# A decode kernel's 30 attention units: written out, and as a loop of 15 rounds

## The chip, the cores and the metric

The kernel runs on one core of one Trainium2 chip. The core has five engines that run side by side, each with its own instruction queue: TensorE (PE, matrix multiplies; its weight loads are listed as PEld), VectorE (DVE), ScalarE (ACT), GpSimd (POOL) and SyncE (SP, which here only issues loads and stores). Sixteen DMA engines move data between HBM and the on-chip memory. The metric is device time in microseconds (us), the median of several runs: 1339.32 us before the change (three runs, 1339.19 to 1339.5).

## What is computed

One decode step: an attention block over a long key/value cache and a small MLP block on the same input, mixed by a gate. Cut to what matters:

```python
def reference(A_x, A_k_cache, A_v_cache, A_wq, A_wo, B_x, B_w1, ..., gate_w):
    # x: (2, 1, 1024); k_cache, v_cache: (2, 32, 16384, 128); wq: (1024, 4096); wo: (4096, 1024)
    x = A_x
    g = sigmoid((x * gate_w).sum(-1, keepdims=True))
    q = (x @ wq) split into 32 heads of 128
    p = softmax(einsum("bhqd,bhkd->bhqk", q, k_cache) * 128 ** -0.5)
    a = einsum("bhqk,bhkd->bhqd", p, v_cache) joined over heads @ wo
    b = x1 + gelu(layernorm(x1) @ w3) @ w4      # x1 = x + shifted gelu(layernorm(x) @ w1) @ w2
    return g * a + (1 - g) * b
```

All inputs are bf16. K and V are 268 MB each, and every byte of them is read once.

## The kernel before

**Units.** The attention is cut into 32 units. A unit is a pair of heads `hp` (0 to 15) of one batch row `b` (0 or 1), in the order `units` (line 88): unit u is pair u // 2 of batch u % 2. Its K is 8 MB and its V is 8 MB, each loaded by one DMA of 128 rows of 64 KB (`load_k`, line 96; `load_v`, line 99).

**Memory.** One tile `mem` of five cells of 32 KB per partition holds the caches: K of even units in cells 0 and 1, K of odd units in cells 1 and 2, V in cells 3 and 4. So the next K may be loaded when the half of the current K that lies in the shared cell 1 has been used, and the next V when the current V has been used. V of unit 30 goes to cells 0 and 1, since no K follows there.

**One unit's work.** `write_qw` (291, POOL) writes the query into a zero-padded weight tile. `score_chunks` (446) goes over K in eight chunks: DVE transposes a chunk (line 454, tile KT, two buffers), PE multiplies it (line 460, 8 matmuls a chunk, into S). `score_first` takes the half in the shared cell, `score_second` the other. `softmax_a` (478) transposes S and takes maxima; `softmax_b` (488) joins the maxima over a matmul and takes exponentials on ACT into the tile Pt; `softmax_c` (509) sums and inverts into rinv. `pv` (543) multiplies Pt with V, 64 matmuls on line 535; `pv_end` (567) scales, reduces, and stores the result in OT; for batch 1 it also projects the pair with `wo` (`wo_project`, line 430), adding to `arow` in PSUM.

**The order.** The loop over units (line 623) is a Python loop, so it is written out in full in the program. In turn n it issues: score_first(n); the load of K(n+1); score_second(n); softmax_a(n); pv(n-2); the load of V(n-1); pv_end(n-2); softmax_b(n); softmax_c(n); and in every fourth turn the `wo` rows of two pairs (`load_wo_pair`, 418). Turns 0 and 1 have pieces of the MLP in place of pv. The last turn loads V of unit 31 in nine pieces (`load_v_pieces`, 105), and `wo` of the last two pairs in four loads (`load_wo_last`, 424). After it come pv and pv_end of unit 30, `pv_last` of unit 31 (595), and the output (663 to 666). A scheduler places waits on semaphores and may move an instruction ahead of others of its engine when it is ready sooner. All loads are issued from SP, in order, on one queue.

Of the kernel before, what the change touches and what calls it, by code (L numbers as in the profile page):

```python
# [1 line left out]

# [1 line left out]

# [7 lines left out]
BF16 = mybir.dt.bfloat16  # L12
ACTF = mybir.ActivationFunctionType
ALU = mybir.AluOpType
# [9 lines left out]
def kernel(  # L24
# [65 lines left out]
    def cache_rows(cache, u):  # L90
# [2 lines left out]
            "(p j) d -> p (j d)", p=P  # L93
        )

    def load_k(u):
        nc.sync.dma_start(out=region(k_cell[u], NJ * Dh), in_=cache_rows(A_k_cache, u))

# [18 lines left out]
    def v_view(u):  # L117
        return region(v_cell[u], NJ * Dh).rearrange("p (j d) -> p j d", d=Dh)
# [169 lines left out]
    lin3.load()  # L288
    qdu = qd[:].rearrange("p hp b v -> p (hp b) v")

    def write_qw(u):
        t = qw[u % NW]
        dst = t[:, :, NG - 1 : NG - 1 + QP * (Q4 - 1) + 1 : QP]
        nc.gpsimd.tensor_tensor(  # L294
            out=dst,
            in0=qdu[:, u, :].unsqueeze(2).to_broadcast([P, 4, Q4]),
            in1=mask4[:].unsqueeze(1).to_broadcast([P, 4, Q4]),
            op=ALU.mult,
        )
# [102 lines left out]

    OT = const.tile([P, HP, 2, B], BF16)
    LASTP = 2
    wo_pairs = A_wo.rearrange("(hp p r) n -> p hp (r n)", p=P, r=2)
    wo_heads = A_wo.rearrange("(h d) n -> d h n", d=Dh)
    wo_tiles = {}

    def wo_tile(hp0):
        t = wopool.tile([P, 2, 2, D], BF16, name="wo")
        for k in range(2):
            for r in range(2):
                wo_tiles[hp0 + k, r] = t[:, k, r, :]
        return t

    def load_wo_pair(hp0):
        t = wo_tile(hp0)
        nc.sync.dma_start(  # L420
            out=t[:].rearrange("p k r n -> p k (r n)"), in_=wo_pairs[:, hp0 : hp0 + 2, :]
        )

    def load_wo_last():
        t = wo_tile(HP - LASTP)
        for k in range(2):
            for r in range(2):
                nc.sync.dma_start(out=t[:, k, r, :], in_=wo_heads[:, H - 4 + 2 * k + r, :])

    def wo_project(hp):  # L430
        for r in range(2):
            for k in range(NH2):
                nc.tensor.matmul(  # L433
                    arow[k],
                    lhsT=OT[:, hp, r, :],
                    rhs=wo_tiles[hp, r][:, k * 512 : (k + 1) * 512],
                    start=False,
                    stop=(hp == HP - 1 and r == 1),
                    skip_group_check=True,
                )  # L440

    S_tiles = {}
    st_tiles = {}
# [2 lines left out]
    def score_chunks(u, chunks, first, last):  # L446
        if first:
            S_tiles[u] = sps.tile([P, GT * QP], FP32, name="S")
        S = S_tiles[u][:].rearrange("p (j k) -> p j k", k=QP)
        t = qw[u % NW]  # L450
        for n, c in enumerate(chunks):
            Kc = k_view(u)[:, c * CT : (c + 1) * CT, :]
            kt = ktpool.tile([P, CT * Dh // 2], FP32, name="KT")
            nc.vector.transpose(out=kt[:], in_=Kc.rearrange("p j d -> p (j d)").bitcast(FP32))  # L454
            ktb = kt[:].bitcast(BF16).rearrange("p (j w k e) -> p j w k e", j=CT, w=2, k=QP, e=2)
            for half in range(CT // GT):
                m = c * (CT // GT) + half
                for v in range(4):
                    w, e = divmod(v, 2)
                    nc.tensor.matmul(  # L460
                        S,
                        lhsT=t[:, v, NG - 1 - m : NG - 1 - m + P],
                        rhs=ktb[:, half * GT : (half + 1) * GT, w, :, e],
                        start=(first and n == 0 and half == 0 and v == 0),
                        stop=(last and n == len(chunks) - 1 and half == CT // GT - 1 and v == 3),
                    )
# [1 line left out]

    half_chunks = [list(range(NCK // 2)), list(range(NCK // 2, NCK))]

    def score_first(u):
        write_qw(u)
        score_chunks(u, half_chunks[1 - k_cell[u]], True, False)

    def score_second(u):
# [12 lines left out]
    def softmax_b(u):  # L488
        st, Dm = st_tiles.pop(u)
        R_ps = misc_psum([P, P])  # L490
        nc.tensor.matmul(R_ps[:], lhsT=ones_f[:], rhs=Dm[:], start=True, stop=True)  # L491
# [15 lines left out]
        rs_tiles[u] = rs  # L507
# [22 lines left out]

    def pv_moving(u, g0, g1, ng):
        acc = oacc[u % 2]
        for g in range(g0, g1):
            q = g % Q4
            nc.tensor.matmul(  # L535
                acc[QP * q : QP * q + 8, :],
                lhsT=pts[u % NP][:, g].rearrange("p h k -> p (h k)"),
                rhs=v_view(u)[:, 4 * g : 4 * g + 4, :].rearrange("p j d -> p (j d)"),
                start=(g < Q4),
                stop=(g >= ng - Q4),  # L540
            )

    def pv(u):
        pv_moving(u, 0, NJ // 4, NJ // 4)
# [22 lines left out]
    def pv_end(u):  # L567
        hp, b = units[u]
        mask = stat.tile([P, 4], FP32, name="maskr")
        nc.vector.tensor_scalar(  # L570
            out=mask[:], in0=mask4m[:], scalar1=rinvs[u % NP][:, 0:1],
            scalar2=g_rep[:, b : b + 1], op0=ALU.mult, op1=ALU.mult,
        )
        red = pv_rows(u, mask)
        if hp >= HP - LASTP:
            ot = misc_psum([P, 2])
            nc.tensor.matmul(ot[:], lhsT=red[:, 0:Dh], rhs=hsel[:], start=True, stop=True)
            nc.vector.tensor_copy(out=OT[:, hp, :, b], in_=ot[:])
            return
        ot = misc_psum([P, 2, 2])  # L580
        for r in range(2):
            nc.tensor.matmul(  # L582
                ot[:, r, :],
                lhsT=red[:, r : 2 * Dh : 2],
                rhs=hsel[:],
                start=True,
                stop=True,
            )
        for e in range(2):
            rows = slice(e * HALF, (e + 1) * HALF)  # L590
            nc.vector.tensor_copy(out=OT[rows, hp, :, b], in_=ot[rows, :, e])  # L591
        if b == B - 1:
            wo_project(hp)

    def pv_last(u):
        hp, b = units[u]
# [5 lines left out]
        for j in range(4 * moving, NJ):  # L602
# [4 lines left out]
                start=(j == 4 * moving),  # L607
                stop=False,
            )
        for k in range(HP - LASTP, HP - 1):  # L610
            wo_project(k)
        nc.tensor.matmul(ot[:], lhsT=red[:, 0:Dh], rhs=hsel[:], start=False, stop=True)
        nc.vector.tensor_tensor(out=OT[:, hp, :, b], in0=ot[:], in1=rinvs[u % NP][:], op=ALU.mult)
        wo_project(HP - 1)

    compute_gate()
    layernorm_T(xT[:], xn1T[:], "ln1")
# [2 lines left out]
    lin2.compute()  # L620
    mlp_post2()

    for n in range(NU):
        score_first(n)
        if n + 1 < NU:
            load_k(n + 1)
        else:
            load_v(NU - 2)
        score_second(n)
        softmax_a(n)  # L630
        if n == 0:
            load_wo_pair(0)
# [5 lines left out]
        elif n == 1:  # L638
# [5 lines left out]
        else:  # L644
            pv(n - 2)
            if n < NU - 1:
                load_v(n - 1)
            else:
                load_v_pieces(NU - 1)
            pv_end(n - 2)  # L650
            if n == NU - 1:
                load_wo_last()
            softmax_b(n)
            softmax_c(n)
        if n % 4 == 1 and 1 < n < NU - 3:
            load_wo_pair((n - 1) // 2)
    pv(NU - 2)
    pv_end(NU - 2)
    pv_last(NU - 1)

    out_row = mlp.tile([QP + B, 512], BF16)
    rows = out.rearrange("b s d -> (b s) d")
    nc.vector.tensor_copy(out=out_row[0:B, :], in_=arow[0])  # L663
    nc.sync.dma_start(out=rows[:, 0:512], in_=out_row[0:B, :])
    nc.scalar.activation(out=out_row[QP : QP + B, :], in_=arow[1], func=ACTF.Copy)
    nc.scalar.dma_start(out=rows[:, 512:1024], in_=out_row[QP : QP + B, :])


# [28 lines left out]
```

## Time and profile before

| | |
|---|---|
| median of 3 runs | 1339.32 us |
| the profiled execution: its time | 1339.11 us |
| the profiled execution: its span | 1337.4 us |
| HBM read | 572.53 MB, 428 GB/s over the span |
| granted TensorE clock, mean | 0.776 |
| K loads, issue to landing (median of 32) | 28.3 us |
| V loads, issue to landing (median of 31) | 33.3 us |

How to read the rows that follow: "busy us, mean ns, idle before, releaser" tells how long a group of instructions ran, how long one took, and what ended the idle time of its engine before it. In a timeline each row has its start and its length in us from the start of the span, the engine, the line and the operation, out<-in, and in brackets the idle time before it. SPq is SP's queue, where DMAs are issued. "q1" and so on are DMA queues: q1 carries the data, q8 and q14 carry instructions to the engines; their rows have packets, MB and the share of 16 engines' span. A row of a chain has start, length and what ran. A row of windows has a stretch, its length, busy time and count of PE, PEld, DVE, ACT and POOL, then the granted clock, the busy share of the DMA engines and GB/s.

### The profile page before, as it was taken

How to read it: one execution, taken by the hardware profiler on the slowest of the kernel's cores; microseconds unless marked ns; L12 is line 12 of the kernel's file. 1: busy time of each engine (PE TensorE's matmuls, PEld its weight loads, DVE VectorE, ACT ScalarE, POOL GpSimd, SP SyncE). 2: the span in 40 equal slices, each digit the busy share in tenths (PEclk: the TensorE clock that was granted, in tenths of full speed). 3: DMA queues.
4: the chain of work that ended last, by engine and by line, in shares of the span. 5: the costliest groups of instructions: out<-in, count | busy, mean ns of one | idle time of the engine just before them, and what ended most of it. 6: DMA issues, size and time to landing. Idle time of an engine off the chain costs nothing.

```text
span 1337.4 us, 11166 instructions
## 1 busy us (share of the span) xinstructions
PE 753.6 (56%) x4842; PEld 314.7 (24%) x4842; DVE 711.9 (53%) x700; ACT 106.9 (8%) x169; POOL 13.9 (1%) x49
## 2 busy tenths in 40 slices
PE   2456566554566645556655546665455765545664
PEld 1223222221222222222222212222222222222221
DVE  2455566553556654456555445656455665545561
ACT  0011000000000000000000000000000000000000
POOL 1000000000000000000000000000000000000000
PEclk9678888776788767788777778877678887778886
DMA  9999999999999999999999999999999999999997
GB/s 408 436 423 440 428 434 432 436 426 437 434 430 440 423 434 432 438 438 420 438 424 438 436 434 434 420 435 430 441 428 432 436 422 430 436 436 432 426 431 321
DMA packets 14041, 573.25 MB, mean 429 GB/s; under 512 B 1828, under 2 KB 1832, under 8 KB 4392
## 3 DMA queue, kind: packets, MB, share of 16 engines
q1 hardware_dynamic: 13988, 572.54, 99.4%
q8 instruction: 38, 0.62, 0.2%
q14 instruction: 11, 0.09, 0.0%
q10 hardware_dynamic: 4, 0.00, 0.0%
HBM read 572.53 MB, written 0.00 MB: 428 GB/s over the span
## 4 chain that ended last, share of the span: by engine, by line
DMA 73%; PE 12%; DVE 12%; issue 4%; SPq 0%
DMA mem<-in_A_k_cache_dram 70%; DVE KT L454 11%; PE S L460 11%; DMA mem<-in_A_v_cache_dram 2%; DMA wo<-in_A_wo_dram 1%; PE oacc L535 0%; SPq L217 0%; DVE out_row L663 0%; PE arow L433 0%; SPq L125 0%; SPq L123 0%; SPq L121 0%
## 5 line engine op out<-in xcount | busy, mean ns | idle before, releaser
L460 PE MATMUL S<-KT,qw 128*128 128x512 bf16 x2048 | 548.4, 418 | 385.8 <-DVE KT L454 385.4
L454 DVE STREAM_TRANSPOSE KT<-mem 128x2048 f32<-128x2048 f32 x256 | 570.9, 2282 | 285.2 <-DMA mem<-in_A_k_cache_dram 234.6
L460 PEld LDWEIGHTS <-qw 128*128 128x128 bf16 x2048 | 219.0, 107 | 710.4 <-issue 531.9
L535 PE MATMUL oacc<-mem,pt 128*8 128x512 bf16 x2040 | 120.1, 387 | 13.3 <-DMA mem<-in_A_v_cache_dram 13.3
L499 ACT ACTIVATE pt<-St,nb 64x256 bf16<-64x256 f32 x64 | 89.7, 1402 | 151.8 <-DVE nb L497 150.9
L485 ACT ACTIVATE Dm<-ident_s,m 128x128 f32<-128x128 f32 x32 | 12.9, 402 | 1003.0 <-DVE m L483 1003.0
L513 PE MATMUL misc<-rs,lmat 128*128 128x1 f32 x62 | 18.2, 363 | 87.7 <-ACT pt L499 87.7
L535 PEld LDWEIGHTS <-pt 128*8 128x8 bf16 x2040 | 47.3, 87 | 82.4 <-issue 31.6
L515 DVE RECIPROCAL rinv<-misc 128x1 f32<-128x1 f32 x31 | 5.2, 168 | 100.1 <-PE misc L513 100.1
L481 DVE STREAM_TRANSPOSE St<-S 128x512 f32<-128x512 f32 x32 | 22.9, 717 | 65.6 <-PE S L460 65.6
L551 DVE TENSOR_SCALAR part<-oacc,maskr 128x128 f32<-128x128 f32 x31 | 10.9, 351 | 83.1 <-PE oacc L535 83.1
L582 PE MATMUL misc<-hsel,red 128*128 128x2 f32 x112 | 17.2, 258 | 51.6 <-DVE red L557 51.6
L513 PEld LDWEIGHTS misc<-rs,lmat 128*128 128x128 f32 x62 | 15.5, 311 | 101.6 <-ACT pt L499 101.6
L582 PEld LDWEIGHTS misc<-hsel,red 128*128 128x128 f32 x112 | 15.6, 199 | 64.9 <-issue 64.9
L499 ACT ACTIVATION_READ_ACCUMULATOR pt<-St,nb 64x1 f32 x64 | 30.5, 477 | 0.0
L557 DVE SCALAR_TENSOR_TENSOR part<-oacc,maskr,part 128x128 f32<-128x128 f32 x62 | 21.8, 351 | 2.2
L274 PE MATMUL oacc<-mem,xT 128*2 128x512 bf16 x128 | 8.3, 426 | 23.4 <-DVE xT L265 23.4
L591 DVE CAST OT<-misc 64x2 bf16<-64x2 f32 x56 | 9.0, 160 | 22.7 <-PE misc L582 22.3
L294 POOL TENSOR_TENSOR qw<-qd,mask 128x16 bf16<-128x16 bf16 x32 | 8.5, 267 | 1189.0 <-PE S L460 1165.9
L491 PE MATMUL misc<-Dm,ones_f 128*128 128x128 f32 x64 | 16.7, 346 | 1.8 <-ACT Dm L485 1.8
L497 DVE TENSOR_REDUCE nb<-misc 64x1 f32<-64x64 f32 x64 | 14.2, 222 | 4.6 <-PE misc L491 2.9
L557 DVE SCALAR_TENSOR_TENSOR red<-oacc,maskr,part 128x256 f32<-128x256 f32 x31 | 15.0, 484 | 1.1
(97 smaller groups left out, 114.4 us busy)
## 6 DMA issues: line engine op xcount, KB each, us to landing
mem<-in_B_w_dram SPq DMA_DIRECT2D x2, 7168.0 KB, 35.1
wo<-in_A_wo_dram SPq DMA_DIRECT2D x7, 1024.0 KB, 31.8
mem<-in_A_v_cache_dram SPq DMA_DIRECT2D x7, 1024.0 KB, 23.5
mem<-in_B_w_dram SPq DMA_DIRECT2D x2, 2048.0 KB, 31.2
mem<-in_A_v_cache_dram SPq DMA_DIRECT2D x2, 512.0 KB, 17.9
wo<-in_A_wo_dram SPq DMA_DIRECT2D x4, 256.0 KB, 12.8
mem<-in_A_k_cache_dram SPq DMA_DIRECT2D x32, 28.3
mem<-in_A_v_cache_dram SPq DMA_DIRECT2D x31, 33.3
```

Of the source, the lines that this page charges most:

```text
L454: nc.vector.transpose(out=kt[:], in_=Kc.rearrange("p j d -> p (j d)").bitcast(FP32))
L460: nc.tensor.matmul(S, lhsT=t[:, v, NG - 1 - m : NG - 1 - m + P], rhs=ktb[:, half * GT : (half + 1) * GT, w, :, e], start=(first and n == 0 ...
L481: nc.vector.transpose(out=st[:].rearrange("p j r -> p (j r)"), in_=S[:])
L485: nc.scalar.activation(out=Dm[:], in_=ident_s[:], func=ACTF.Copy, scale=m[:, 0:1])
L491: nc.tensor.matmul(R_ps[:], lhsT=ones_f[:], rhs=Dm[:], start=True, stop=True)
L497: nc.vector.tensor_reduce(out=nb[rows], in_=R_ps[rows, rows], axis=AX.X, op=ALU.min)
L499: nc.scalar.activation(out=Pt[rows, :, e, :].rearrange("p (m a) k -> p a k m", a=GT // 4), in_=st[rows, :, 0:NG].rearrange("p (a k) m -> p ...
L513: nc.tensor.matmul(tot_ps[:, 0:1], lhsT=lmat[:], rhs=rs[:], start=True, stop=True)
L535: nc.tensor.matmul(acc[QP * q : QP * q + 8, :], lhsT=pts[u % NP][:, g].rearrange("p h k -> p (h k)"), rhs=v_view(u)[:, 4 * g : 4 * g + 4, ...
L551: nc.vector.tensor_scalar(out=part[:], in0=acc[:, 0:Dh], scalar1=mask[:, 0:1], scalar2=None, op0=ALU.mult)
L557: nc.vector.scalar_tensor_tensor(out=red[:] if twice else part[:], in0=in0.unsqueeze(1).to_broadcast([P, 2, Dh]) if twice else in0, scalar ...
L582: nc.tensor.matmul(ot[:, r, :], lhsT=red[:, r : 2 * Dh : 2], rhs=hsel[:], start=True, stop=True,)
```

## The change

Units 0 and 1 stay written out. Units 2 to 31 become a loop of 15 rounds on the chip, i from 0 to 14, with a register as counter. A round has two units: 2 + 2i, and 3 + 2i. The second unit stands in an `If`: in rounds 0 to 13 the first arm runs it; in round 14 the `Else` arm runs unit 31 with all that followed the loop before, the output too. With `iteration_sync="reg_based"` the loop does not stop the engines between rounds to reset semaphores: the semaphores only grow, and a wait in the body compares with a register that is raised in each round. `hint_engines=()` asks for no branch hints.

```diff
+    pairs = {
+        "k": [cache_pairs(A_k_cache, b) for b in range(B)],
+        "v": [cache_pairs(A_v_cache, b) for b in range(B)],
+    }
+    def load_pair(cell, cache, hp, b):
+        src = pairs[cache][b][bass.ds(hp, 1)].rearrange("o p x -> (o p) x")
+        nc.sync.dma_start(out=region(cell, NJ * Dh), in_=src)
...
-    NP = 4
+    NP = 2
...
-    def write_qw(u):
+    def write_qw(u, at=None):
         t = qw[u % NW]
+        q = qdu[:, u, :] if at is None else qdu[:, bass.ds(at, 1), :].rearrange("p o v -> p (o v)")
...
-    OT = const.tile([P, HP, 2, B], BF16)
-    LASTP = 2
+    OT = const.tile([P, 2, B], BF16, name="OT")
+    OT_last = const.tile([P, 2, B], BF16, name="OT_last")
...
+    wo_now = wopool.tile([P, 2, D], BF16, name="wo")
+    def load_wo(hp):
+        src = wo_pairs[hp] if isinstance(hp, int) else wo_pairs[bass.ds(hp, 1)].rearrange(
+            "o p x -> (o p) x"
+        )
+        nc.sync.dma_start(out=wo_now[:].rearrange("p r n -> p (r n)"), in_=src)
     def load_wo_last():
-        t = wo_tile(HP - LASTP)
-        for k in range(2):
-            for r in range(2):
-                nc.sync.dma_start(out=t[:, k, r, :], in_=wo_heads[:, H - 4 + 2 * k + r, :])
+        for r in range(2):
+            nc.sync.dma_start(out=wo_now[:, r, :], in_=wo_heads[:, H - 2 + r, :])
...
+    queued = [None]
+    def behind():
+        return tc.issue_after(queued[0].ins) if queued[0] is not None else nullcontext()
...
-    for n in range(NU):
+    for n in range(2):
...
+    def unit_first(b, i):
+        u = 2 + b
+        score_first(u, 2 * i + u)
+    def unit_second(b):
+        u = 2 + b
+        score_second(u)
+        softmax_a(u)
+        pv(b)
+    def unit_end(b):
+        u = 2 + b
+        pv_end(b)
+        softmax_b(u)
+        softmax_c(u)
...
+    with tc.For_i(0, HP - 1, 1, hint_engines=(), iteration_sync="reg_based") as i:
+        queued[0] = None
+        unit_first(0, i)
+        load_pair(k_cell[1], "k", i + 1, 1)
+        unit_second(0)
+        load_pair(v_cell[1], "v", i, 1)
+        unit_end(0)
+        with tc.If(i < HP - 2) as more:
+            queued[0] = None
+            unit_first(1, i)
+            nxt = nc.s_assert_within(
+                i + 2, 2, HP - 1, skip_runtime_bounds_check_because="this arm has i < HP - 2"
+            )
+            load_pair(k_cell[2], "k", nxt, 0)
+            unit_second(1)
+            load_pair(v_cell[2], "v", i + 1, 0)
+            unit_end(1)
+            load_wo(i + 1)
+        with more.Else():
+            n = NU - 1
+            queued[0] = None
+            score_first(n)
+            load_v(n - 1)
+            score_second(n)
+            softmax_a(n)
+            pv(n - 2)
+            load_v_pieces(n)
+            pv_end(n - 2)
+            load_wo_last()
+            softmax_b(n)
+            softmax_c(n)
+            pv(n - 1)
+            pv_end(n - 1)
+            pv_last(n)
+            nc.vector.tensor_copy(out=out_row[0:B, :], in_=arow[0])
...
```

With it come four smaller edits. The addresses of K, V and `wo` in HBM, and of the query, are worked out from the counter (`load_pair`, `load_wo`, `write_qw`); K and V are viewed by pairs of heads, with the same 128 rows of 64 KB. `wo` is loaded one pair at a time, in each round, into one tile; the last pair alone is loaded in the order by heads, in two loads. Pt and rinv have two buffers instead of four, and OT one pair. The matmuls of `pv_moving`, and softmax_b's, are pinned behind the last matmul queued on PE before them (`behind`), where before the scheduler's own order held.

More of the change, by code (lines that the diff above doesn't have):

```diff
@@ L1 @@
-from contextlib import ExitStack
+from contextlib import ExitStack, nullcontext
 import numpy as np
@@ L459, in score_chunks @@
                     w, e = divmod(v, 2)
-                    nc.tensor.matmul(
+                    queued[0] = nc.tensor.matmul(
                         S,
@@ L490, in softmax_b @@
         R_ps = misc_psum([P, P])
-        nc.tensor.matmul(R_ps[:], lhsT=ones_f[:], rhs=Dm[:], start=True, stop=True)
+        with behind():
+            nc.tensor.matmul(R_ps[:], lhsT=ones_f[:], rhs=Dm[:], start=True, stop=True)
         nb = stat.tile([P, 1], FP32, name="nb")
@@ L532, in pv_moving @@
         acc = oacc[u % 2]
[L533 to L541, printed above, removed]
+        with behind():
+            for g in range(g0, g1):
+                q = g % Q4
+                last = nc.tensor.matmul(
+                    acc[QP * q : QP * q + 8, :],
+                    lhsT=pts[u % NP][:, g].rearrange("p h k -> p (h k)"),
+                    rhs=v_view(u)[:, 4 * g : 4 * g + 4, :].rearrange("p j d -> p (j d)"),
+                    start=(g < Q4),
+                    stop=(g >= ng - Q4),
+                )
+        queued[0] = last
     def pv(u):
@@ L590, in pv_end @@
             rows = slice(e * HALF, (e + 1) * HALF)
[L591 removed]
+            nc.vector.tensor_copy(out=OT[rows, :, b], in_=ot[rows, :, e])
         if b == B - 1:
[L593 removed]
+            wo_project(OT, wo_now)
     def pv_last(u):
@@ L637 @@
             softmax_c(n)
-        elif n == 1:
+        else:
             lin4.compute()
@@ L662 @@
[L662 to L666, printed above, removed]
+            pv(n - 1)
+            pv_end(n - 1)
+            pv_last(n)
+            nc.vector.tensor_copy(out=out_row[0:B, :], in_=arow[0])
+            nc.sync.dma_start(out=rows[:, 0:512], in_=out_row[0:B, :])
@@ L670 @@
+            nc.scalar.activation(out=out_row[QP : QP + B, :], in_=arow[1], func=ACTF.Copy)
+            nc.scalar.dma_start(out=rows[:, 512:1024], in_=out_row[QP : QP + B, :])
 _INS = ['A_x', 'A_k_cache', 'A_v_cache', 'A_wq', 'A_wo', 'B_x', 'B_w1', 'B_w2', 'B_w3', 'B_w4', 'gate_w']
```

63 lines of the change are left out of this document (20 added, 43 removed).

## The prediction

> **What bounds the kernel now.** I read the page's head, its slices and DMA queues first, then the chain that ended last, then one unit in the order of time.
>
> ```profile
> span 1337.4 us, 11166 instructions
> ...
> PE 753.6 (56%) x4842; PEld 314.7 (24%) x4842; DVE 711.9 (53%) x700; ACT 106.9 (8%) x169; POOL 13.9 (1%) x49
> ...
> DMA  9999999999999999999999999999999999999997
> ...
> q1 hardware_dynamic: 13988, 572.54, 99.4%
> q8 instruction: 38, 0.62, 0.2%
> q14 instruction: 11, 0.09, 0.0%
> ...
> DMA mem<-in_A_k_cache_dram 70%; DVE KT L454 11%; PE S L460 11%; DMA mem<-in_A_v_cache_dram 2%; DMA wo<-in_A_wo_dram 1%; PE oacc L535 0%; SPq L217 0%; DVE out_row L663 0%; PE arow L433 0%; SPq L125 0%; SPq L123 0%; SPq L121 0%
> ```
>
> The data queue q1 keeps all 16 DMA engines busy for 99.4% of the span, and the chain is mostly the landing of K. No compute engine passes 56%. So an edit counts if it changes the work of the DMA engines, or if it is late enough to leave their queue empty. How late that is shows in one unit (issue and landing of its loads, and the work between):
>
> ```profile
> 903.75 0.33 SPq L100 DMA_DIRECT2D mem<-in_A_v_cache_dram  x1
> ...
> 907.62 0.38 SPq L420 DMA_DIRECT2D wo<-in_A_wo_dram  x1
> ...
> 917.40 4.50 DVE L454 STREAM_TRANSPOSE KT<-mem 128x2048 f32<-128x2048 f32 x2 [6.58 <-DMA mem<-in_A_k_cache_dram]
> ...
> 927.90 0.33 SPq L97 DMA_DIRECT2D mem<-in_A_k_cache_dram  x1
> ...
> 942.20 0.33 SPq L100 DMA_DIRECT2D mem<-in_A_v_cache_dram  x1
> ...
> 949.47 0.29 DVE L570 TENSOR_SCALAR maskr<-mask4m,rinv,g_rep 128x4 f32<-128x4 f32 x1
> 958.73 4.50 DVE L454 STREAM_TRANSPOSE KT<-mem 128x2048 f32<-128x2048 f32 x2 [8.98 <-DMA mem<-in_A_k_cache_dram]
> 961.10 5.37 PE L460 MATMUL S<-KT,qw 128*128 128x512 bf16 x16 [11.87 <-DVE KT L454]
> ```
>
> ```profile
> mem<-in_A_v_cache_dram SPq DMA_DIRECT2D x31, 33.3
> ```
>
> K lands at 917.40, the work on it ends at 949.76 (949.47 + 0.29), so it takes 32.4 us, and DVE then idles 8.98 us until the next K. There is a second cover behind that: the next K load is issued at 927.90, while the V load issued at 903.75 lands at about 903.75 + 33.3 = 937.05. For 9.15 us the queue still has data, and a K load may be that late before a DMA engine starves. For the V load it is 958.73 - 942.20 = 16.5 us.
>
> How even is the pace? The starts of the first transpose after each K landing, in the chain:
>
> ```profile
> 128.60 2.32 DVE KT L454
> ...
> 403.61 2.32 DVE KT L454
> ...
> 442.31 2.32 DVE KT L454
> ...
> 483.60 2.32 DVE KT L454
> ...
> 561.02 2.32 DVE KT L454
> ...
> 600.96 2.32 DVE KT L454
> ...
> 838.64 2.32 DVE KT L454
> ...
> 878.50 2.32 DVE KT L454
> ...
> 1154.88 2.32 DVE KT L454
> ...
> 1194.74 2.32 DVE KT L454
> ...
> 1272.44 2.32 DVE KT L454
> ```
>
> The DMA queues and loads between 128.60 and 1272.44, and the instructions before, in and after that stretch:
>
> ```profile
> q8 instruction: 32, 0.52, 0.2%
> ...
> wo<-in_A_wo_dram SPq DMA_DIRECT2D x6, 1024.0 KB, 32.1
> ```
>
> ```profile
> 0.00:128.60 128.60, 59.73 (x546) 27.66 (x547) 56.03 (x90) 10.05 (x18) 6.38 (x21) 0.81 0.99 425
> 128.60:1272.44 1143.84, 656.80 (x3998) 272.52 (x3998) 630.12 (x580) 93.06 (x145) 7.48 (x28) 0.77 1.00 432
> 1272.44:1337.40 64.96, 37.02 (x298) 14.49 (x297) 25.76 (x31) 3.79 (x6) 0.00 (x0) 0.74 0.89 375
> ```
>
> A plain unit takes 442.31 - 403.61 = 38.70 us, one with a wo load 483.60 - 442.31 = 41.29, or 2.59 more. Units 2 to 31 start 29 units apart: 29 x 38.70 + 6 x 2.59 = 1137.8, against 1143.84 measured. **6.0 us are left over**, and not evenly: 561.02 to 600.96 is 39.94, 838.64 to 878.50 is 39.86, 1154.88 to 1194.74 is 39.86, three steps of about 1.2 us, 278 and 316 us apart. Those are candidates for instruction fetch. The first two columns of counts are PE's matmuls and weight loads: 9684 instructions in all, and 9684 / 38 packets is 255 per packet of q8, so q8 carries PE's program, one packet every 35 us. Eight packets are 282 us, about the distance of the steps: I read it as one DMA engine receiving every eighth packet and landing its share of K and V later each time. A packet costs that engine 0.2% x 16 x 1337.4 / 38 = 1.13 us (0.84 to 1.41 with the rounding of 0.2%), which is the size of a step. A K load has landed when its slowest engine has, so the steps add up.
>
> **The change, part by part.** *Instructions removed from the stream.* Units 2 to 30 hold 7996 PE instructions, 276 per unit, 551 per round, 2.2 packets. In the loop each round runs the same code. If PE keeps it after the first round, fetches are 1093 / 256 = 4.3 for the start, 2.2 for one round and 595 / 256 = 2.3 for the other arm: about 9 instead of 38, and about 30 of the stretch's 32 are gone. By share of the left-over that is 6.0 x 30 / 32 = 5.6 us; by the visible steps alone 3 x 1.2 = 3.6, or 2.4 if one of the last arm's fetches brings a step back. I take the middle of 3.6 and 5.6, rounded down, **-4.5 us**, ends -2.4 and -6.0. If PE does not keep it, see the rivals.
>
> *Loop control* (counter, compare, two taken branches per round and engine, register additions, addresses for SP and POOL). No row shows one. Lower end 0; upper end by the nearest small instruction, L570's 0.29 us: 30 per round are 8.7 us on an engine. A taken branch may wait for code: 1.13 us of packet at least, at most also a 2 KB transfer's whole trip (the output's issue at 1335.02 to the end at 1337.4, 2.4 us): 3.5 each, 7 per round.
>
> ```profile
> 1335.02 0.33 SPq L664 DMA_DIRECT2D out_dram<-out_row  x1
> ```
>
> I take 0 for the end time, because it falls where DVE idles 8.98 us and PE 11.87 before the next K, 38.70 - 32.4 = 6.3 in a unit without a wo load, and the K load can then slip 9.15 more. Both ends added, 8.7 + 7 = 15.7, just use up 6.3 + 9.15 = 15.4; with that cover gone each us more costs 15. What is late in such a case is first the transpose, then the K load, then on SP's queue the V load and the wo load behind it.
>
> *Waits against registers.* They replace waits on constants at the same places if they are as exact. Behind a waiting K load on SP stand V and wo; behind a waiting transpose on DVE stands the rest of its chain. Exact: 0. Inexact: a rival.
>
> *Loads.* K and V keep their rows, size, cells and order. Seven wo loads of 1 MB and four of 256 KB become fifteen of 512 KB and two of 256 KB: the same bytes, 6 more issues at 0.38 us on an SP that is idle from 907.62 to 927.90. 0.
>
> *Two Pt and rinv buffers instead of four, and PE's order pinned behind the last queued matmul.* The exponentials of a unit already come after PV of the unit two before (V's issue at 942.20 follows that PV). maskr may move from 949.47 into the next unit: 0.29 us in DVE's idle time. 0.
>
> *The end.* Four projection matmuls leave the tail, but the chain there hangs on the last wo load (1% of the span), and the bytes ahead of it are the same. Between 0 and -1.1 (half of the last projections' 2.27); I take 0, since the load comes last.
>
> ```profile
> 1332.01 2.27 PE L433 MATMUL arow<-wo,OT 128*2 128x512 bf16 x8
> ```
>
> Sum: the profiled execution took 1339.11 (span 1337.4 and 1.7 around it), and the median is 1339.32, 0.2 above. 1339.3 - 4.5 = **1334.8 us**.
>
> [...]
>
> **The rivals.** (1) *Fetch stays as it is*: each round fetches its 2 to 3 blocks anew, hidden as now. For it: q8 runs at one packet per 256 instructions all through, so nothing in this trace shows code being kept. Nothing else changes: 1337 to 1341, about 1339.
>
> [...]
>
> (3) *Waits across rounds are coarser*: a K load that waits for the V load ahead of it leaves the queue empty from 937.05 for the trip of a new load, about 2.4 us. Once per round +36, 1375; in each unit +70, 1409. For it: the arms of a branch must meet in one state. Against it: a counter per engine can be exact.
>
> (4) *Control eats the cover*: over 15.4 us per round end; 3 us more give +45, 1384. Against it: that needs both upper ends at once.
>
> **How the numbers follow.** Forecast 0.45, rival 1 0.17, rival 2 0.23, rival 3 0.10, rival 4 0.05. The forecast's own range is 1333 to 1337. The whole range runs to rival 2's 1352 with room for a few more packets, 1332.8 to 1356; rivals 3 and 4 are left out. A measurement of this kernel can tell about 0.2%, 2.7 us, so faster means below 1336.6: nearly all of the forecast, 0.42. Same takes the forecast's upper edge and rival 1, 0.20. Slower, above 1342, takes the rest, 0.38.
>
> **What would show it.** Right: q8 with about 9 to 12 packets, K landings 38.70 apart without steps, q1 still at 99% or more, DVE's idle time before K still there at each round's end. Wrong: q8 at 38 or more (rivals 1, 2), a K landing later than 38.7 once per round, or a slice of the DMA row below 9 in the loop (rivals 3, 4).

## The result, and the profile after

| | median us | lowest to highest, runs |
|---|---|---|
| before | 1339.32 | 1339.15 to 1339.84, 11 |
| after | 1335.85 | 1335.69 to 1336.59, 11 |

The ratio is 0.9974, with a 95% interval of 0.9965 to 0.9984: 3.5 us faster. The forecast was 1334.8. The profiled execution after the change has a span of 1334.2 us, 3.2 less than before. Its page:

```profile
span 1334.2 us, 13326 instructions
...
PE 761.0 (57%) x4846; PEld 321.2 (24%) x4846; DVE 709.0 (53%) x702; ACT 107.0 (8%) x169; POOL 12.8 (1%) x47
...
q1 hardware_dynamic: 13956, 572.54, 99.5%
q8 instruction: 11, 0.18, 0.1%
```

The DMA engines are as full as before, and the engines do the same work but for the loop's control. What has gone is code on its way to PE: 11 packets in place of 38 (before, 9684 / 38 is 255 PE instructions to a packet). When they come is told by the DMA queues in three stretches, 0 to 210 us, 210 to 1290 and 1290 to the end (packets, MB, share):

```profile
q8 instruction: 8, 0.13, 0.3%
```

```profile
q1 hardware_dynamic: 9920, 467.67, 100.2%
```

```profile
q8 instruction: 3, 0.05, 0.4%
```

The middle answer has no row for q8 at all. From 210 us on, 5 us into the second of the 15 rounds, PE runs up to the last arm without one packet of code, and that arm, which no round has run before, brings three. The pace of K in the chain of waits, one row per round (rows between are left out):

```profile
362.81 2.32 DVE KT L467
...
441.48 2.32 DVE KT L467
...
834.90 2.32 DVE KT L467
...
913.58 2.32 DVE KT L467
...
1268.20 2.32 DVE KT L467
```

A round takes 441.48 - 362.81 = 78.67 us, and 78.68 half a millisecond later. Two plain units and half a wo load of before are 2 x 38.70 + 1.30 = 78.70. The steps are gone, and the loop's own control is not to be seen in the pace. The first row after that jump back, in the order of time, shows why:

```profile
913.58 4.50 DVE L467 STREAM_TRANSPOSE KT<-mem 128x2048 f32<-128x2048 f32 x2 [5.94 <-DMA mem<-in_A_k_cache_dram]
```

DVE still stands idle for 5.94 us across the jump back (in brackets), and what ends that is the landing of K, not the jump. Then the middle stretch and the end (length, then busy time and count of PE, PEld, DVE, ACT, POOL, then clock, DMA share, GB/s), with PE's code and the wo loads of the middle one, from its DMA view:

```profile
127.56:1268.20 1140.64, 663.95 (x4000) 278.82 (x4000) 627.32 (x581) 93.05 (x145) 7.43 (x28) 0.77 1.00 433
1268.20:1334.20 66.00, 37.66 (x300) 15.10 (x299) 26.33 (x34) 3.79 (x6) 0.00 (x0) 0.71 0.87 370
```

```profile
q8 instruction: 4, 0.07, 0.0%
...
wo<-in_A_wo_dram SPq DMA_DIRECT2D x14, 512.0 KB, 29.4
```

| stretch | before | after | difference |
|---|---|---|---|
| start to the K of unit 2 | 128.60 | 127.56 | -1.04 |
| K of unit 2 to K of unit 31 | 1143.84 | 1140.64 | -3.20 |
| K of unit 31 to the end | 64.96 | 66.00 | +1.04 |

By the pace worked out for before (38.70 a plain unit, 2.59 per MB of wo) the middle stretch would take 29 x 38.70 + 14 x 1.295 = 1140.4. So of the 6.0 us that were left over before, 0.2 remain. But 7 MB of wo lie in the stretch now and 6 did before, which gives 2.6 back. The end is longer. Its last rows after, and the matching two before:

```profile
1327.94 0.59 PE L619 MATMUL misc<-pt,mem 128*128 128x2 bf16 x16 [0.66 <-DMA mem<-in_A_v_cache_dram]
...
1330.43 0.68 DVE L712 CAST out_row<-arow 2x512 bf16<-2x512 f32 x1 [1.16 <-PE arow L440]
...
1331.14 0.34 SPq L713 DMA_DIRECT2D out_dram<-out_row  x1
```

```profile
1331.07 0.58 PE L603 MATMUL misc<-pt,mem 128*128 128x2 bf16 x16 [0.69 <-DMA mem<-in_A_v_cache_dram]
...
1334.31 0.68 DVE L663 CAST out_row<-arow 2x512 bf16<-2x512 f32 x1 [2.03 <-PE arow L433]
```

From the last K to the last piece of V: 58.63 before (1331.07 - 1272.44), 59.74 after, +1.11. From there to the cast: 3.24 and 2.49, -0.75. From the cast to the end: 3.09 and 3.77, +0.68. Three theories were to be told apart: the gain is code that is no longer fetched; the gain comes from one of the small edits; and, for the end, the arm's own code or the loop's exit brings something back.

### The profile page after: what moved, and what is told of

The parts are those of the page before. It is cut to its first block, busy times and chain, and to the rows that moved or that the text cites. A ratio compares the mean times of both kernels' runs of the same rounds, so it can differ in the third digit from the quotient of the medians.

```text
span 1334.2 us, 13326 instructions
## 1 busy us (share of the span) xinstructions
PE 761.0 (57%) x4846; PEld 321.2 (24%) x4846; DVE 709.0 (53%) x702; ACT 107.0 (8%) x169; POOL 12.8 (1%) x47
## 3 DMA queue, kind: packets, MB, share of 16 engines
q1 hardware_dynamic: 13956, 572.54, 99.5%
## 4 chain that ended last, share of the span: by engine, by line
DMA 65%; PE 13%; DVE 11%; issue 6%; another core or an unknown queue 1%; PEld 0%; DVEq 0%; SPq 0%; PEldq 0%; POOL 0%
DMA mem<-in_A_k_cache_dram 61%; PE S L473 12%; DVE KT L467 11%; DMA mem<-in_A_v_cache_dram 3%; PE oacc L550 1%; PEld L473 0%; DVEq L467 0%; DVE part L573 0%; SPq L109 0%; PE arow L440 0%; DVE red L573 0%; PEld misc L598 0%; DVE part L567 0%; POOL ln_rstd L359 0%
## 5 line engine op out<-in xcount | busy, mean ns | idle before, releaser
L473 PEld LDWEIGHTS <-qw 128*128 128x128 bf16 x2048 | 216.1, 106 | 687.1 <-issue 510.0
L598 PE MATMUL misc<-hsel,red 128*128 128x2 f32 x120 | 20.3, 274 | 70.8 <-DVE red L573 70.8
L598 PEld LDWEIGHTS misc<-hsel,red 128*128 128x128 f32 x120 | 18.6, 219 | 85.1 <-issue 85.1
L505 PE MATMUL misc<-Dm,ones_f 128*128 128x128 f32 x64 | 19.8, 403 | 1.8 <-ACT Dm L498 1.8
L511 DVE TENSOR_REDUCE nb<-misc 64x1 f32<-64x64 f32 x64 | 14.2, 222 | 6.8 <-PE misc L505 3.5
```

The lines of the kernel that those rows point to most:

```text
L473: queued[0] = nc.tensor.matmul(S, lhsT=t[:, v, NG - 1 - m : NG - 1 - m + P], rhs=ktb[:, half * GT : (half + 1) * GT, w, :, e], start=(firs ...
L598: nc.tensor.matmul(ot[:, r, :], lhsT=red[:, r : 2 * Dh : 2], rhs=hsel[:], start=True, stop=True,)
```

## The experiments

Times of the kernel before in these runs were 1339.25, 1339.21 and 1339.19, so the runs can be set side by side.

**The small edits without the loop.** All of the change, but with the rounds written out.

```diff
-    with tc.For_i(0, HP - 1, 1, hint_engines=(), iteration_sync="reg_based") as i:
+    for i in range(HP - 1):
...
-        with tc.If(i < HP - 2) as more:
+        if i < HP - 2:
...
-        with more.Else():
+        else:
```

> The 15 rounds written out again, with every other edit of the change kept (loads by pairs, one wo pair per round, two Pt buffers, PE's order pinned). Fetch theory (the gain is the instruction packets of PE that no longer pass through the DMA engines): q8 back at about 38 packets, steps of about 1.2 us in the K landings, 1339 us, between 1338.3 and 1340. Rival, the smaller edits made the gain: q8 at 38 and still 1336 us.

Measured: 1339.77, ratio 1.0003 (0.9994 to 1.0012). The page's row of PE's code, the windows (split at the K of units 2 and 31), and two rows of the chain:

```profile
q8 instruction: 38, 0.62, 0.2%
```

```profile
127.49:1273.87 1146.38, 654.24 (x4000) 271.95 (x4000) 630.20 (x580) 93.02 (x145) 7.46 (x28) 0.78 1.00 432
1273.87:1338.00 64.13, 37.64 (x300) 14.85 (x299) 25.93 (x32) 3.80 (x6) 0.00 (x0) 0.71 0.87 366
```

```profile
837.46 2.32 DVE KT L467
...
917.29 2.32 DVE KT L467
```

This kernel has the same loads in the same stretch as the changed one, the same work on every engine but for the loop's control, and 38 packets. Its middle stretch is 1146.38 - 1140.64 = **5.74 us longer**. And the steps are back: the round shown takes 79.83 us (917.29 - 837.46), where the loop has 78.67. The gain is the loop's, and the small edits together cost 1338.0 - 1337.4 = 0.6 us of span: -1.1 in the start and -0.8 in the end, where less wo lies, and +2.5 in the middle, where more does.

**What a packet costs, and rounds with twice the code.** Two kernels get 128 tiny matmuls (2x2, into a spare PSUM tile) more in each unit from 2 to 30: one with the rounds written out, one in the loop. The expectations take 0.19 us a packet, the 6.0 us left over in the middle stretch of before by its 32 packets.

```diff
+    def dummies():
+        t = misc_psum([2, 2])
+        with behind():
+            for _ in range(128):
+                nc.tensor.matmul(t[:], lhsT=mask4[:, 0:2], rhs=mask4[:, 0:2], start=True, stop=True)
...
     def unit_end(b):
...
         softmax_c(u)
+        dummies()
```

Written out:

> The written-out rounds with 128 tiny matmuls (2x2) more on PE at the end of each of units 2 to 30: 7424 PE instructions more, 29 packets, into a scratch tile that nothing reads. Fetch theory: q8 at about 67 and 29 x 0.19 = 5.5 us more than the same without them, about 1344.5 (1342 to 1348). Rival, PE's time counts and not the packets: it is off by what the same matmuls cost in the loop.

In the loop:

> The changed kernel (loop) with the same 128 tiny matmuls more at the end of each of units 2 to 30. They run on PE as often as in the written-out kernel, but stand in the program once per unit of a round, 2 packets. Fetch theory: q8 at 12 to 15, 1336 to 1337 us, since PE idles some 9 us there. Rival, PE's time counts: the same rise as in the written-out kernel, 3 us or more.

Measured: written out 1345.69, ratio 1.0048 (1.0034 to 1.0062); in the loop 1335.99, ratio 0.9976 (0.9967 to 0.9985). The pages, PE's code written out and then PE's work and code in the loop:

```profile
q8 instruction: 67, 1.10, 0.3%
```

```profile
PE 932.8 (70%) x8558; PEld 494.1 (37%) x8558; DVE 708.9 (53%) x702; ACT 107.0 (8%) x169; POOL 12.8 (1%) x47
...
q8 instruction: 13, 0.21, 0.1%
```

The same extra work costs 1345.69 - 1339.77 = 5.92 us where its code is fetched, in 29 more packets, or **0.20 us a packet**, and nothing where it is not (1335.99 against 1335.85). The 7424 PE instructions more (2 x 3712) are 256 to each of the 29 packets, near the 255 of before. So it is the packets, not PE's busier time. That agrees with the loop: 28 packets fewer in the middle stretch (4 by its DMA queues, against 32) for 5.74 us, 0.205 each. In that pair seven of q14's packets, of 8 KB each, go too (3 in the middle stretch against 10); in the other pair q14 has 11 in both. And the loop with the extra matmuls has 551 + 512 = 1063 matmuls and weight loads a round, 4.2 packets' worth at 256 each, and still ran almost without fetching: between 210 and 1290 us one packet comes.

The 0.20 us is a mean, and the traces show what it is made of. In the kernel before there are four steps and not three. The fourth is a unit with a wo load, so it hides in a longer unit:

```profile
283.71 2.32 DVE KT L454
...
326.12 2.32 DVE KT L454
```

That is 42.41 us, 1.12 more than the 41.29 of such a unit. And here are PE's packets in the DMA queues of that trace, first up to 290 us, then from 290 to 294:

```profile
q8 instruction: 8, 0.13, 0.2%
```

```profile
q8 instruction: 1, 0.02, 1.7%
```

So the ninth packet comes inside the first step. By the same view the 17th comes between 580 and 590 us, the 25th between 860 and 870 and the 33rd between 1165 and 1172, each inside one of the other three steps. With the rounds written out the four steps stand in the same four units (by the chain, 40.96 us from 283.78, 39.70 from 561.11, 40.91 from 837.46 and 40.97 from 1153.67, where such units otherwise take 39.98 and 38.70). With the extra matmuls written out there are eight steps of 1.3 to 1.5 us, most of them 159 us apart, and eight of its 67 packets are 160 us of the span. So one packet in eight makes a step of some 0.9 to 1.5 us (less than 0.1 is left in the mean for each of the others). The trace does not name the DMA engine that moves a packet; that it is the same one at each step was the author's reading, and is not shown.

**Rounds with more code.** Three and five rounds are written out in one turn of the loop, which leaves four jumps back or two. The small query multiplication of the loop (line 310) runs on DVE in these two, 0.18 to 0.22 us per unit.

```diff
-    with tc.For_i(0, HP - 1, 1, hint_engines=(), iteration_sync="reg_based") as i:
+    with tc.For_i(0, HP - 1, 3, hint_engines=(), iteration_sync="reg_based") as i0:
...
-        eng = nc.gpsimd
+        eng = nc.gpsimd if at is None else nc.vector
```

Three rounds a turn; the question is whether PE holds the code of a whole turn until the next one:

> Three rounds per turn, five turns: 1653 PE instructions and some control per turn, 6.5 to 7 packets' worth (write_qw in the loop on DVE). [...] If it holds less, the code is missed at each of four back edges as it was with five rounds per turn: q8 at 36 or more, and some 7 to 8 us lost per edge, 1362 to 1372.

Five rounds a turn:

> Five rounds per turn of the loop, three turns: 2755 PE instructions and some control per turn, 11 packets' worth, instead of 551. write_qw in the loop runs on DVE instead of POOL. Fetch theory with a limit to the code that PE keeps: if it holds less than 11 packets, each turn is fetched anew, q8 at 36 to 42, 1338.5 to 1340 us. If it holds that much: q8 at about 20 and 1336 to 1337.5. Rival, the gain is the loop's as such and not fetch: 1336 with q8 at 38.

Measured: three rounds 1357.43, ratio 1.0134 (1.0117 to 1.0151); five rounds 1355.34, ratio 1.0116 (1.0101 to 1.0132). Both are slower than before. With five rounds all three expected ranges were missed; with three, the range for a turn that is not held, 1362 to 1372 us, was too high. The five rounds' page:

```profile
GB/s 403 431 438 439 432 432 424 433 434 430 432 436 430 430 432 392 374 429 426 432 438 434 432 421 432 442 432 355 417 434 430 434 427 434 432 432 434 429 432 305
...
q8 instruction: 48, 0.79, 0.3%
```

Inside the loop the data rate falls at two places, in slices 16 and 17 (508 to 576 us) and 28: the two jumps back. Three rounds' page, its DMA queues between 360 and 1260 us, and its first jump back in the order of time:

```profile
q8 instruction: 57, 0.93, 0.3%
```

```profile
q8 instruction: 42, 0.69, 0.3%
q14 instruction: 19, 0.16, 0.1%
```

```profile
365.99 2.31 DVE L468 STREAM_TRANSPOSE KT<-mem 128x2048 f32<-128x2048 f32 x1 [9.04 <-issue]
...
373.17 7.92 PE L474 MATMUL S<-KT,qw 128*128 128x512 bf16 x24 [16.43 <-issue]
```

A turn has 3 x 551 = 1653 PE instructions or 6.5 packets' worth here, and is fetched anew each time: 11 packets come in each 240 us or so of a turn (42 in these 900 us), more than the 6.5, and more than the 8.8 with the last arm. On q14 packets come too, 19 against 3 in the changed kernel's middle stretch. At the jump DVE and PE wait for nothing that the profile shows ("issue"), PE until 4.87 us after the first transpose had ended (373.17 - 368.30) and 4.76 after the write of the query that follows it (at 368.41). Between 345 and 385 us five of PE's packets come, and in the changed kernel not one between 895 and 935, around a jump there; so a wait for code fits, and is not shown. Packets alone do not make the loss: 46 more than the changed kernel's 11 at 0.204 are 9.4 us, and 1357.43 - 1335.85 is 21.6. The other 12.2, or 3 us for each jump, and 6 for each of the two by the same sum for five rounds (19.5 less 37 x 0.204, halved), are put down to the jumps; the 23 packets that q14 has more (27 against 4), of 8 KB each, are in it. Whether that is work which waited for code, or many packets close together on few DMA engines, was not separated. What the query's move to DVE adds was not run alone, but between two jumps it is not to be seen: two units take 39.97 and 38.70 us there (from 445.88 to 524.55), as in the changed kernel. Each turn also has one step of some 1.0 us, at the same unit each time (40.91 to 40.95 in the last four turns, where the changed kernel has 39.9), 241 to 242 us apart, which is about 11 packets. So a step may go with a packet's place in the program rather than with the count. Taken together, 1063 PE instructions a round ran with one packet between 210 and 1290 us, and 1653 a turn with 42 between 360 and 1260, both with an arm of 595 to jump over. No run lies between the two, and none shows whether the arm counts.

**Hints at the jump back.** The changed kernel with the loop's default hints.

```diff
-    with tc.For_i(0, HP - 1, 1, hint_engines=(), iteration_sync="reg_based") as i:
+    with tc.For_i(0, HP - 1, 1, iteration_sync="reg_based") as i:
```

> The changed kernel, but with the loop's default hints to the engines' instruction fetch at the back edge. Theory (after the first round all of a round's code is kept, so there is nothing left to fetch ahead): 1335.5 to 1336.5 us, as the changed kernel, with 11 to 13 instruction packets on PE's queue. Rival (the hints fetch the loop's head anew in each round): some 14 to 28 packets more at 0.20 us each, 1338 to 1342 us.

Measured: 1335.98, ratio 0.9977 (0.9967 to 0.9986). The page has

```profile
q8 instruction: 9, 0.15, 0.0%
```

two packets fewer than without hints, against the 11 to 13 that were expected, and the time is the same. The loop's head is not fetched anew in each round: between 127.56 and 1268.2 us three packets come, where the kernel without hints has four, and 15 rounds run.

**The cover at the round's end.** DVE gets a chain of transposes of a spare tile at the end of each of rounds 0 to 13, behind rinv: 10 of them, or 20.

```diff
...
             load_wo(i + 1)
+            nc.vector.tensor_copy(out=spare[:, 0:1], in_=rinvs[1][:, 0:1])
+            for _ in range(10):
+                nc.vector.transpose(out=turned[:], in_=spare[:])
```

Ten:

> Ten small transposes of a scratch tile more on DVE at the end of each round but the last, about 9 to 10 us per round, behind the unit's last reciprocal. By the cover of the prediction (DVE idles 6 us there and the K load may then be 9 us late) it costs nothing: 1335.5 to 1337 us. Rival, the kernel has no such cover: +3 us or more per round, 1378 or more.

Twenty:

> Twenty of them, about 18 to 20 us per round. The cover is 6 + 9.15 = 15, less the start of a load (about 2): 3 to 7 us per round stick out, 14 rounds, 1378 to 1434 us. If the cover is larger than thought: 1336.

Measured: ten 1335.88, ratio 0.9975 (0.9966 to 0.9985), which is nothing; twenty 1430.73, ratio 1.0681 (1.0664 to 1.0699). Twenty at one round's end, in the order of time:

```profile
883.32 20.23 DVE L701 STREAM_TRANSPOSE turned<-spare 128x768 f32<-128x768 f32 x20
903.49 4.51 DVE L467 STREAM_TRANSPOSE KT<-mem 128x2048 f32<-128x2048 f32 x2
```

K's transpose follows without idle time: DVE is late, not the load. Twenty take 20.23 us, and 1430.73 - 1335.85 = 94.9 us over 14 rounds is 6.8 a round, within the 3 to 7 that were expected. So 13.4 of the 20.2 were hidden. That is a steep edge: the first ten cost nothing, the second ten 95 us.

**The waits at the round's end.** The changed kernel, with a barrier in place of the waits on growing counts.

```diff
-    with tc.For_i(0, HP - 1, 1, hint_engines=(), iteration_sync="reg_based") as i:
+    with tc.For_i(0, HP - 1, 1, hint_engines=(), iteration_sync="barrier") as i:
```

> The changed kernel, but with all engines and SP meeting at a barrier at the end of each round instead of waits against growing counts. Theory (exact waits are a condition of the gain: whatever lets SP issue the next loads only after the loads in flight have landed empties the data queue): at a round's end SP waits for the landing of all its loads, so the 9 to 10 us of data that the queue held are gone, and a new load's trip of about 2.4 us comes on top: 12 to 14 us per round, 14 rounds, +170 to +200: 1505 to 1535 us, with dips in the data rate every 80 to 90 us. Rival (the round's end has slack for a barrier: 6 us on DVE and 9 in the queue): under 1345 us.

Measured: 1538.84, ratio 1.1491 (1.147 to 1.1512), 4 us over the upper end: 203 us, 14.5 for each of 14 rounds. One round's end:

```profile
940.80 0.33 SPq L431 DMA_DIRECT2D wo<-in_A_wo_dram  x1
...
972.10 4.50 DVE L467 STREAM_TRANSPOSE KT<-mem 128x2048 f32<-128x2048 f32 x2 [28.27 <-PEq L678]
```

DVE stands for 28.27 us, until the wo load issued at 940.80 has landed (30.1 us in this kernel, the median of its page, so at about 970.9). No slack hides that: while the queue drains, from 940.80 to 972.10, no new load is issued.

**The last arm.** In place of an `Else` arm in round 14 the loop has 14 rounds, and units 30 and 31 stand behind it.

```diff
-    with tc.For_i(0, HP - 1, 1, hint_engines=(), iteration_sync="reg_based") as i:
+    with tc.For_i(0, HP - 2, 1, hint_engines=(), iteration_sync="reg_based") as i:
...
-        with tc.If(i < HP - 2) as more:
...
+    i = HP - 2
+    queued[0] = None
+    unit_first(0, i)
...
```

> 14 rounds in the loop, and units 30 and 31 with the output written out behind it: no branch in the body. Theory that the arm is only a matter of code: 2 packets more, the branch gone, 1335 to 1337 us. Theory that leaving the loop is what the arm avoids: at the exit SP waits for every load to land, the queue runs empty for the transposes of half a K and a load's start, 10.5 + 2.4 = 13 us once, 1346 to 1352.

Measured: 1349.54, ratio 1.0076 (1.0059 to 1.0093). The loop's exit in the order of time:

```profile
1218.33 0.33 SPq L431 DMA_DIRECT2D wo<-in_A_wo_dram  x1
...
1249.36 4.50 DVE L467 STREAM_TRANSPOSE KT<-mem 128x2048 f32<-128x2048 f32 x2 [27.81 <-PEq L744]
...
1260.16 0.34 SPq L109 DMA_DIRECT2D mem<-in_A_k_cache_dram  x1
```

The same picture as the barrier's, once: all engines meet behind the loop when the last load has landed (1218.33 + 29.5, the median of its wo loads, is 1247.8), and the next K is issued only at 1260.16. From 1240 to 1270 us the data queue is busy for 52.1%. It costs 1349.54 - 1335.85 = 13.7 us. Up to the K of unit 31 it is 14.2, near the barrier's 14.5 (1282.38 here, 1268.20 in the changed kernel); some comes back at the very end, where the output now stands outside the loop. Putting the last unit into the loop as an arm is what spares that, since the exit then comes after the output.

**A last unit without code of its own.** The second unit's code serves the last unit too; three small `If`s hold what differs.

```diff
+        unit_first(1, i)
         with tc.If(i < HP - 2) as more:
...
             load_pair(k_cell[2], "k", nxt, 0)
-            unit_second(1)
+        with more.Else():
+            load_v(n - 1)
+        unit_second(1)
+        with tc.If(i < HP - 2) as more:
             load_pair(v_cell[2], "v", i + 1, 0)
-            unit_end(1)
+        with more.Else():
+            load_v_pieces(n)
+        pv_end(1)
+        softmax_b(3)
...
+        with tc.If(i < HP - 2) as more:
+            softmax_c(3)
             load_wo(i + 1)
         with more.Else():
...
```

> The changed kernel, but the last unit runs through the same code as the second units of the rounds; three small branches hold only what differs (which load is issued, and the ending). About 270 PE instructions, one packet, fewer have to be fetched late. Theory (the 1.1 us that the last K lands late come from the packets of the last arm's own code, on one DMA engine): 0 to 1.1 us less than the changed kernel, 1334.7 to 1335.9 us. Rival (each branch on SP waits for the landing of the loads of the other arm, so that one K or V load is issued late in each round): 1350 us or more.

Beside it, on the same chip, the changed kernel again:

> The changed kernel itself once more, beside the kernel with the shared last unit and on the same chip: 1335.5 to 1336.3 us.

Measured: 1341.19, ratio 1.0016 (1.0007 to 1.0025), and 1335.88, ratio 0.9975 (0.9966 to 0.9984) for the changed kernel again. Neither theory gave this 5.3 us more. The loop is not slower: the K of unit 31 is worked on from 1268.21, against 1268.20. The end:

```profile
q8 instruction: 8, 0.13, 0.0%
```

```profile
1268.21 4.50 DVE L467 STREAM_TRANSPOSE KT<-mem 128x2048 f32<-128x2048 f32 x2 [7.23 <-DMA mem<-in_A_k_cache_dram]
...
1326.88 3.14 PE L550 MATMUL oacc<-mem,pt 128*8 128x512 bf16 x25 [14.18 <-DMA mem<-in_A_v_cache_dram]
...
1335.82 0.68 DVE L713 CAST out_row<-arow 2x512 bf16<-2x512 f32 x1 [0.74 <-PE arow L440]
```

With no packet in the end (all 8 come before 210 us), the last of V is there 58.67 us after K, as with the rounds written out (58.77, by the row below) and not 59.74 as in the changed kernel. So the arm's packets cost about 1.0 us. They are the 9th to 11th of that kernel. The loop with the extra matmuls has the same arm and 13 packets in all, one of them between 210 and 1290 us, and there the last V comes only 58.98 us after K (1327.88 - 1268.90):

```profile
1268.90 2.32 DVE KT L467
```

```profile
1327.88 0.58 PE L619 MATMUL misc<-pt,mem 128*128 128x2 bf16 x16 [0.68 <-DMA mem<-in_A_v_cache_dram]
```

That most of the 1.0 us belongs to the ninth packet, as in the steps, fits both, but is not shown: when the last packets of the 13 come was not measured. But with the shared code PE no longer takes V piece by piece: it waits 14.18 us and starts only when all pieces are there, and the cast comes 8.94 us after that, in place of 2.49. The pieces are issued inside an `If` that is closed before their use; that the use therefore waits for all of them fits the rows, but was not tested. A version that keeps both, shared code and waits by pieces, was not tried.

The end of the kernel with the rounds written out, for the comparison:

```profile
1332.64 0.58 PE L619 MATMUL misc<-pt,mem 128*128 128x2 bf16 x16 [0.69 <-DMA mem<-in_A_v_cache_dram]
...
1334.96 0.68 DVE L710 CAST out_row<-arow 2x512 bf16<-2x512 f32 x1 [1.11 <-PE arow L440]
...
1335.67 0.33 SPq L711 DMA_DIRECT2D out_dram<-out_row  x1
```

From the output's issue to the end it takes 1338.0 - 1335.67 = 2.33 us here and 2.38 before, but 1334.2 - 1331.14 = 3.06 in the changed kernel and 1339.6 - 1336.52 = 3.08 with the shared unit, the two where the output stands inside the loop. Four other traces agree. From the cast to the end it is 3.92 us with three rounds a turn (1356.7 - 1352.78) and 4.43 with five (1354.2 - 1349.77), where the output stands inside the loop, as in the changed kernel with 3.77; it is 2.95 with the extra matmuls written out (1343.8 - 1340.85) and 3.07 without the arm (1347.6 - 1344.53), where it stands outside, as before the change with 3.09. What takes the time there is not known.

No kernel here beats the changed one.

## Why the prediction was right, point by point

*What bounds the kernel.* Right: 99.5% of q1, and up to the end an edit counted only through the packets or through an empty queue; in the end, once the last loads are on their way, PE's wait for all pieces of V counted too. 172 us more of PE busy time, the tiny matmuls in the loop (932.8 against 761.0), cost nothing (1335.99 us against 1335.85).

*Steps are instruction packets.* Right: 0.20 us of kernel time for each packet as a mean, by two pairs that share one kernel, where the left-over of before gave 0.19 (6.0 / 32). That every eighth packet makes the step was read from size and distance; the packets' times bear it out in the trace of before, and the steps' places and distances in the two kernels with the rounds written out. That one DMA engine gets them all is the author's reading: no trace names it. The prediction missed a step, the one of 1.12 us at 283.71.

*Instructions removed.* The direction and the mechanism were right, the size too careful: -5.74 in the middle stretch. Between the share of the left-over (5.6) and the visible steps (3.6) the middle was chosen, rounded to -4.5; the share was right. The visible steps are four and make 4.7 us, and the other 1.3 of the 6.0 are delays of at most 0.3 in single units. The packets left were 11, not 9. The lower end's condition came true: the arm's packets give a step back, +1.0. Net -4.8 against -4.5. That the two come so close is luck: the gain was put too low by 1.2, and the step that came back, 1.0, was left out of the middle value.

*Loop control.* 0 was right, and the reason too: K's landing still ends DVE's idle time. The cover was put at 15.4 us at a round's end; the twenty transposes found 13.4 left beside the control. The expectation of that run had taken off about 2 us for the start of a load, which leaves nothing for the control; without that it takes some 2 us at most, if 15.4 was exact. The price of a missed branch, 3.5 us at most, was too low if PE's wait at the jump with three rounds a turn is one for code: it starts 4.87 us after its first transpose.

*Waits against registers.* Exact, as assumed: 0 (78.67 us a round, against 78.70 by the pace of before). The price of rival 3 counted one new load's trip, 2.4 us a round. A barrier cost 14.5, but it asks for more: every load has to land, and half of a K has to be transposed, before the next K is issued (10.8 us at the exit without the arm, 1249.36 to 1260.16). A K load that waits for V alone was not run.

*Loads and the end.* Each taken as 0. The bytes are the same in sum, but the middle stretch has 1 MB more, at 2.6 us: half a MB of it comes from the start, where it cost about as much, and half from the end, where it lay behind the last V. The small edits together are +0.6. The end's share of them, from the last V to the cast, is -0.92 with the rounds written out (3.24 and 1334.96 - 1332.64 = 2.32) and -0.75 in the changed kernel, within the stated 0 to -1.1. The 0 was taken because the last wo load comes last; with half of it gone, the chain after hangs on the last V instead. What the prediction did not have is the exit: +0.7 between the output's issue and the end.

Sum, from the spans: -5.74 + 1.0 + 0.6 + 0.7 + 0.2 (last V to cast, loop against written out, 2.49 - 2.32) = -3.2, as measured. By the spans the forecast's -4.5 is 1.3 us off, by the medians 1.0. Its packet term was right in net, by the luck named above; the small terms that it put at 0 are 1.5 together.

*The rivals.* Rival 1 (fetch stays as it is) and rival 2 (more fetch) are refuted by the middle stretch: 4 packets came there in place of 32, and none between 210 and 1290 us. No run shows the term behind rival 2's 1352, from which the whole range's upper end of 1356 comes: from 210 us on the changed kernel's rounds ran without a packet, and 1063 PE instructions a round ran with 13 packets in all. More fetch than before came only with three and five rounds a turn, 57 and 48 packets against 38, and then gave 1357.43 and 1355.34 us. With three rounds a turn the 19 packets more than before are 3.9 us at 0.204 each, of the 18.2 lost.

## What to carry to other kernels

Where the data queue is as full as here (99.4% of the span), fetched code costs time as well: count the instruction packets, price them by a pair of kernels that differ in them (here 0.20 us in the mean, and most of it in every eighth), and try a loop, which saved 27 of 38 here. Keep its body small: here 1063 PE instructions a round still ran with 13 packets, but a turn of 1653 brought 57, and cost them and 3 us at each jump (6 with 2755). And look for every point at which the engines meet: a loop's exit or a barrier in front of a running stream of loads cost 13.7 and 14.5 us here, because no new load was issued while the queue drained. What follows such a loop is better put into its last round, which took 1335.85 us here against 1349.54.

## What the runs showed that was not expected

- A packet of code, 16 KB here (0.62 MB / 38), cost 0.20 us of kernel time in a kernel that moves 429 GB/s, though 16 KB would be 0.04 us by that rate. The cost is not even: with the rounds written out every eighth packet makes a step of 0.9 to 1.5 us in the landing of K.
- A loop's exit with loads in flight cost 13.7 us here, and a barrier 14.5 us per round, against 0 for waits on growing counts.
- An output issued inside the loop ended 0.7 us later (3.06 and 3.08 against 2.33 and 2.38); why is not known.
